# A sparse linear layer on one core: a new opening with six weight pieces, bf16 transposes and in-place pruning

## The chip, the core and the metric

The kernel runs on one core of one Trainium2 chip. The metric is device time in microseconds (us), the median over runs. Engines: TensorE (PE in the profile; its weight loads are listed apart as PEld), VectorE (DVE), ScalarE (ACT), GpSimd (POOL) and SyncE (SP). SyncE and ScalarE also issue the kernel's transfers, each from a queue of its own, in order.

## The reference

```python
B, S, D = 16, 512, 1024
x: (B, S, D) bf16;  w: (D, D) bf16;  b: (D,) bf16

def reference(x, w, b):
    G = D // 4
    wg = w.reshape(G, 4, D)
    mag = jnp.abs(wg)
    order = jnp.argsort(mag, 1)
    thr = jnp.take_along_axis(mag, order[:, 2:3, :], 1)
    mask = (mag >= thr)
    wp = (wg * mask).reshape(D, D)
    return jnp.einsum("bsd,df->bsf", x, wp) + b
```

In every group of four neighbouring rows of w, in each column, the two entries of largest magnitude stay (all that equal the second largest stay too), the others become zero. Then x times the pruned w, plus b. There are 8192 tokens, that is 64 tiles of 128; each tile needs 8 blocks of 128 contraction rows against 1024 output columns, so 16 matmuls of 512 columns.

## The kernel before

**Two layouts.** The rows of w are packed: partition q of half g (g is 0 or 1) holds rows 4q to 4q+3 of that half, as four slices m. So the four entries of a group lie in one partition and VectorE can compare them. The first 7 tiles of tokens are multiplied against this packed pruned weight `wp` while it is being made; this is the *opening*. The pruned weight is also written to a scratch tensor in memory (`save`, L183) and read back in natural row order (`reload`, L186); the other 57 tiles are multiplied against that `wp_nat`, with x brought in by transposing transfers (`load_batch`, L237). That is the *natural part* (L334 and L369). Its first batch, 5 tiles, runs all first output halves (h = 0) and then all second halves (h = 1), so the reload of the second half is wanted only at the sixth group of 8 matmuls.

**The opening.** The weight is pruned in pieces, each a half g and a range of columns, `pieces` (L123): seven, of 128, 128, 256, 256, 256, 512 and 512 columns. A piece takes eight steps: `abs`, `hi` and `lo` (larger and smaller of two pairs), `t1` (smaller of the larger two), `t2` (larger of the smaller two), `thr` (larger of these, the second largest of the four), `mask` (magnitude >= thr), `mult` (weight times mask, written to `wp`). VectorE does them (`Piece.do`, L161); the `abs` of some pieces is ScalarE's (`abs_act`, L158).

For a tile t and half g, `transpose` (L192) turns x with TensorE into PSUM, as fp32 words that hold two bf16 each: two fp32 transposes per tile and half. `copy_xt` (L201) has ScalarE bring it to SBUF. `mm_piece` (L209) then multiplies tile t with piece i, four matmuls (m = 0 to 3) that add up in a PSUM buffer of 512 columns for each tile and output half. `psum_o` has six such buffers, one of them first used by the fillers; `psum_t` has two for the transposes. `stage` (L224) copies a finished first half to SBUF on ScalarE and so frees its buffer; `finish` (L229) adds the bias to both halves on VectorE and stores the tile.

**What sets the order.** `seq` chains the instructions of each engine in the order in which they are emitted. Three lists written by hand, `order` (L249), give that order for TensorE, VectorE and ScalarE: T2a is the transpose of tile 2, half a; C2a its copy; M2.3 tile 2 with piece 3; F2 two filler matmuls on zeros; S2 the staging of tile 2; W5 the save of piece 5 from ScalarE's queue. `run` (L306) merges the lists: a token is emitted once those that it needs have been. Before the lists stand six fillers of 512 columns and three of 128 (L316).

SyncE's queue issues, in order: all early loads (L105 to L120), four saves, the transposed x of batch 0, both reloads, then further batches.

**Names.** x with a range, as `x_4_0` in load_x(4, 6, 0), is the load of tiles 4 and 5, half a.

Of the kernel before, what the change touches and what calls it, by code (L numbers as in the profile page):

```python
# [10 lines left out]
def kernel(  # L11
# [7 lines left out]
    nc = tc.nc  # L19
    P = 128  # L20
    bf16 = mybir.dt.bfloat16
# [11 lines left out]
    FH = 512  # L33
# [13 lines left out]

    const = ctx.enter_context(tc.tile_pool(name="const", bufs=1))
    dram = ctx.enter_context(tc.tile_pool(name="dram", bufs=1, space=bass.MemoryType.DRAM))
    wtmp = ctx.enter_context(tc.tile_pool(name="wtmp", bufs=2))  # L50
    xtp = ctx.enter_context(tc.tile_pool(name="xtp", bufs=NPK))
    stg = ctx.enter_context(tc.tile_pool(name="stg", bufs=NPK))
    xtb = ctx.enter_context(tc.tile_pool(name="xtb", bufs=3))
# [13 lines left out]
    def pe(i):  # L67
        return seq("pe", i)

    def dve(i):  # L70
        return seq("dve", i)

    def act(i):
        return seq("act", i)
# [3 lines left out]

    zeros = const.tile([P, P], bf16)
    dve(nc.vector.memset(zeros[:], 0.0))  # L80
    spark = const.tile([P, 1], bf16)


    w_sb = const.tile([P, G, 4, Dout], bf16)
# [9 lines left out]
    def load_w(g, c0, c1, eng="sp"):  # L94
        issue(eng, w_sb[:, g, :, c0:c1], wv[:, g, :, c0:c1])

    def load_x(ta, tb, g, eng="sp"):
        xs = const.tile([P, tb - ta, HK], bf16, name=f"x_{ta}_{g}")
        issue(eng, xs[:], xv[:, ta:tb, g * HK:(g + 1) * HK])
        for t in range(ta, tb):  # L100
            x_sb[(t, g)] = xs[:, t - ta, :]


    act(nc.scalar.activation(spark[:], zeros[:, :1], Act.Abs))
    load_w(0, 0, CW)  # L105
    load_x(0, 1, 0)
    load_x(1, 2, 0)
    load_x(2, 4, 0)
    load_w(0, CW, FH)
    load_x(4, 6, 0)  # L110
    load_w(1, 0, CW)
    load_x(0, 2, 1)
    load_x(2, 4, 1)
    load_x(6, 7, 0)
    load_w(1, CW, FH)
    load_x(4, 6, 1)
    load_x(6, 7, 1)
    load_w(0, FH, Dout)
    load_w(1, FH, Dout)
    sp(nc.sync.dma_start(bias_sb[:], b.partition_broadcast(P)))  # L120


    pieces = [(0, 0, P), (0, P, CW), (0, CW, FH), (1, 0, CW), (1, CW, FH), (0, FH, Dout), (1, FH, Dout)]  # L123

    ident = const.tile([P, P], fp32)
    make_identity(nc, ident[:])
    warm_ps = psum_o.tile([P, FH], fp32, name="ps")

    def filler(n, rep=1):
        for _ in range(n):  # L130
            pe(nc.tensor.matmul(warm_ps[:, :rep * P], lhsT=zeros[:],  # L131
                                rhs=zeros[:, None, :].to_broadcast([P, rep, P]), start=True, stop=True))
# [6 lines left out]

    class Piece:  # L140


        def __init__(self, i):
            self.g, self.c0, self.c1 = pieces[i]
            n = self.n = self.c1 - self.c0
            self.w = w_sb[:, self.g, :, self.c0:self.c1]
            self.mag = wtmp.tile([P, 4, FH], bf16, name="mag", bufs=5)[:, :, :n]
            self.hi = wtmp.tile([P, 2, FH], bf16, name="hi")[:, :, :n]
            self.lo = wtmp.tile([P, 2, FH], bf16, name="lo")[:, :, :n]
            self.t1 = wtmp.tile([P, FH], bf16, name="t1")[:, :n]  # L150
            self.t2 = wtmp.tile([P, FH], bf16, name="t2")[:, :n]
            self.thr = wtmp.tile([P, FH], bf16, name="thr")[:, :n]
            self.mask = wtmp.tile([P, 4, FH], bf16, name="mask")[:, :, :n]

        def tt(self, out, a, b_, op):
            dve(nc.vector.tensor_tensor(out, a, b_, op=op))  # L156

        def abs_act(self):  # L158
            act(nc.scalar.activation(self.mag, self.w, Act.Abs))  # L159

        def do(self, *steps):  # L161
            magv = self.mag.rearrange("p (a j) f -> p a j f", j=2)
            for step in steps:
                if step == "abs":
                    dve(nc.vector.tensor_single_scalar(
                        self.mag.bitcast(u16), self.w.bitcast(u16), 0x7FFF, op=Alu.bitwise_and))
                elif step == "hi":
                    self.tt(self.hi, magv[:, :, 0, :], magv[:, :, 1, :], Alu.max)
                elif step == "lo":
                    self.tt(self.lo, magv[:, :, 0, :], magv[:, :, 1, :], Alu.min)  # L170
                elif step == "t1":
                    self.tt(self.t1, self.hi[:, 0, :], self.hi[:, 1, :], Alu.min)
                elif step == "t2":
                    self.tt(self.t2, self.lo[:, 0, :], self.lo[:, 1, :], Alu.max)
                elif step == "thr":
                    self.tt(self.thr, self.t1, self.t2, Alu.max)
                elif step == "mask":
                    self.tt(self.mask, self.mag,
                            self.thr[:, None, :].to_broadcast([P, 4, self.n]), Alu.is_ge)
                else:  # L180
                    self.tt(wp[:, self.g, :, self.c0:self.c1], self.w, self.mask, Alu.mult)

    def save(g, c0, c1, eng="sp"):  # L183
        issue(eng, scr_pk[:, g, :, c0:c1], wp[:, g, :, c0:c1])
# [7 lines left out]
    def transpose(t, g):  # L192


        xg = x_sb[(t, g)].bitcast(fp32).rearrange("p (q u) -> p u q", u=2)
        tp = psum_t.tile([P, 2, P], fp32, name="tp")
        for u in range(2):
            pe(nc.tensor.transpose(tp[:, u, :], xg[:, u, :], ident[:]))  # L198
        xpk[(t, g)] = tp

    def copy_xt(t, g):  # L201
        xt = xtp.tile([P, 2, P], fp32, name=f"xt{g}")
        act(nc.scalar.copy(xt[:], xpk[(t, g)][:]))  # L203
        v = xt[:].bitcast(bf16).rearrange("p u (t v) -> p u v t", v=2)
        xpk[(t, g)] = [v[:, m // 2, m % 2, :] for m in range(4)]

    ps_open = {}

    def mm_piece(t, i):  # L209
        g, c0, c1 = pieces[i]  # L210
        h = c0 // FH
        new = (t, h) not in ps_open
        if new:
            ps_open[(t, h)] = psum_o.tile([P, FH], fp32, name="ps")
        ps = ps_open[(t, h)]
        for m in range(4):
            pe(nc.tensor.matmul(ps[:, c0 - h * FH:c1 - h * FH], lhsT=xpk[(t, g)][m],  # L217
                                rhs=wp[:, g, m, c0:c1],
                                start=(new and m == 0), stop=(g == 1 and m == 3),
                                skip_group_check=True))  # L220

    staged = {}
# [14 lines left out]
    def load_batch(bi):  # L237
# [5 lines left out]
        for j in range(nb):  # L243
# [4 lines left out]

    order = {  # L249
        "pe": (  # L250
            "T0a T1a F2 T2a T3a F2 M0.0 M1.0 M2.0 M3.0 T4a T5a M0.1 M1.1 M2.1 M3.1 M4.0 M4.1 T0b "
            "T1b M5.0 M5.1 T2b T6a M0.2 T3b M1.2 M2.2 T4b M3.2 T5b T6b M4.2 M5.2 M0.3 M1.3 M2.3 "
            "M3.3 M4.3 M5.3 M0.4 M1.4 M2.4 M3.4 M4.4 M5.4 M6.0 M6.1 M6.2 M6.3 M6.4 M0.5 M1.5 M2.5 "
            "M3.5 M4.5 M5.5 M0.6 M1.6 M2.6 M3.6 M4.6 M5.6 M6.5 M6.6"
        ),
        "dve": (
            "abs0 hi0 lo0 t10 t20 hi1 thr0 lo1 mask0 t11 mult0 t21 thr1 mask1 mult1 abs2 hi2 lo2 "
            "t12 t22 thr2 mask2 mult2 hi3 lo3 t13 t23 thr3 mask3 mult3 hi4 lo4 t14 t24 thr4 mask4 "
            "mult4 hi5 lo5 t15 t25 thr5 mask5 mult5 hi6 lo6 t16 t26 thr6 mask6 mult6"
        ),  # L260
        "act": (
            "abs1 C0a C1a C2a C3a C4a C5a abs3 C0b C1b C2b C6a abs4 C3b C4b C5b C6b abs5 abs6 S0 S1 "
            "S2 S3 S4 S5 W5 S6 W6"
        ),
    }
    written = set()
    p = {}

    def needs(eng, tok):

        if tok[0] == "C":
            return ["T" + tok[1:]]
        if tok[0] in "TF":
            return []
        if tok[0] == "M":
            t, i = tok[1:].split(".")
            return [f"C{t}{'ab'[pieces[int(i)][0]]}", f"mult{i}"]
        if tok[0] == "S":
            return [f"M{tok[1:]}.{i}" for i in range(5)]
        if tok[0] == "W":  # L280
            return ["mult" + tok[1:]]
        return ["abs" + tok[-1]] if tok[:-1] in ("hi", "mask") else []

    def emit(eng, tok):
        if tok[0] == "T":
            transpose(int(tok[1]), "ab".index(tok[2]))
        elif tok[0] == "F":
            filler(int(tok[1:]))
        elif tok[0] == "C":
            copy_xt(int(tok[1]), "ab".index(tok[2]))  # L290
        elif tok[0] == "M":
            mm_piece(*map(int, tok[1:].split(".")))
        elif tok[0] == "S":
            stage(int(tok[1:]))
        elif tok[0] == "W":
            save(*pieces[int(tok[1:])], eng="act")
        else:
            i = int(tok[-1])
            if i not in p:
                p[i] = Piece(i)  # L300
            if eng == "act":
                p[i].abs_act()
            else:
                p[i].do(tok[:-1])

    def run(queues):  # L306
        while any(queues.values()):
# [6 lines left out]
            assert moved, queues  # L314

    filler(6, 4)  # L316
    filler(3)
    run({eng: order[eng].split() for eng in order})
    save(0, 0, CW)
    save(0, CW, FH)  # L320
    save(1, 0, CW)
    save(1, CW, FH)
    load_batch(0)
    reload(0)
    reload(1)
    load_batch(1)
    load_batch(2)
    for t in range(NPK):
        finish(t)


# [76 lines left out]
```

## Time and profile before

| what | value |
|---|---|
| median of 4 runs | 237.25 us (236.18 to 238.4) |
| profiled execution | 236.18 us, span 234.4 us |
| TensorE busy | 228.0 us, 97% of the span |
| VectorE busy | 104.7 us, 45% |
| ScalarE busy | 15.8 us, 7% |
| granted TensorE clock | 1.000 |
| first pruning step, first opening matmul | 3.92 us, 7.03 us |
| first matmul of the natural part | 34.70 us |
| last product of the pruning ready | 26.96 us |
| second reload issued | 32.16 us |

Times inside the run count from the start of the span. A matmul's listed duration reaches from its issue to its modelled end, so neighbours overlap: a 512-wide one is listed with 379 ns while they start 216 ns apart. What TensorE can do is therefore read from the distance of starts, and the share of busy time says only that it hardly waits. A row such as `L198 PE MATMUL tp<-ident,x 128*128 128x128 f32 x28` names line, engine, operation, the tile written and the tiles read, and how many there are.

### The profile page before, as it was taken

How to read it: one execution, taken by the hardware profiler on the slowest of the kernel's cores; microseconds unless marked ns; L12 is line 12 of the kernel's file. 1: busy time of each engine (PE TensorE's matmuls, PEld its weight loads, DVE VectorE, ACT ScalarE, POOL GpSimd, SP SyncE). 2: the span in 40 equal slices, each digit the busy share in tenths (PEclk: the TensorE clock that was granted, in tenths of full speed). 3: DMA queues.
4: the chain of work that ended last, by engine and by line, in shares of the span. 5: the costliest groups of instructions: out<-in, count | busy, mean ns of one | idle time of the engine just before them, and what ended most of it. 6: DMA issues, size and time to landing. Idle time of an engine off the chain costs nothing.

```text
span 234.4 us, 2830 instructions
## 1 busy us (share of the span) xinstructions
PE 228.0 (97%) x1145; PEld 112.2 (48%) x1165; DVE 104.7 (45%) x182; ACT 15.8 (7%) x28; POOL 0.7 (0%) x6
## 2 busy tenths in 40 slices
PE   6899999999999999999999999999999999999995
PEld 3898444444444444444444444444444444444443
DVE  3989697342442442343343244234334324424424
ACT  4588000000000000000000000000000000000000
POOL 1000000000000000000000000000000000000000
PEclk9999999999999999999999999999999999999999
DMA  5999969999999712892219912595221221222122
GB/s 157 316 348 249 339 195 329 313 297 249 262 277 221 241 72 89 206 286 92 89 60 215 301 65 78 117 277 187 92 91 45 89 91 50 86 89 88 49 90 90
DMA packets 79500, 40.29 MB, mean 172 GB/s; under 512 B 60416, under 2 KB 71936, under 8 KB 79488
## 3 DMA queue, kind: packets, MB, share of 16 engines
q1 hardware_dynamic: 68352, 22.45, 43.7%
q10 hardware_dynamic: 11136, 17.67, 21.1%
q8 instruction: 9, 0.15, 0.3%
q14 instruction: 3, 0.02, 0.0%
HBM read 6.29 MB, written 18.87 MB: 107 GB/s over the span
## 4 chain that ended last, share of the span: by engine, by line
PE 95%; DMA 2%; SPq 1%; issue 1%; DVE 0%
PE ps L369 75%; PE ps L217 10%; PE ps L334 9%; DMA x<-in_x_dram 2%; PE tp L198 1%; SPq L92 1%; DVE o L338 0%
## 5 line engine op out<-in xcount | busy, mean ns | idle before, releaser
L369 PE MATMUL ps<-wp_nat,xb 128*128 128x512 bf16 x800 | 175.4, 379 | 0.8
L338 DVE TENSOR_TENSOR o<-ps,bias_sb 128x512 bf16<-128x512 f32 (+1 forms) x116 | 74.3, 678 | 120.5 <-PE ps L369 103.9
L369 PEld LDWEIGHTS <-xb 128*128 128x128 bf16 x816 | 79.9, 98 | 96.3
L217 PE MATMUL ps<-wp,xt 128*128 128x256 bf16 (+2 forms) x194 | 25.4, 287 | 0.1
L334 PE MATMUL ps<-wp_nat,xb 128*128 128x512 bf16 (+2 forms) x110 | 21.0, 348 | 0.1
L217 PEld LDWEIGHTS <-xt 128*128 128x128 bf16 x196 | 17.1, 98 | 7.3
L334 PEld LDWEIGHTS <-xb 128*128 128x128 bf16 x112 | 10.4, 98 | 10.7
L198 PE MATMUL tp<-ident,x 128*128 128x128 f32 x28 | 5.4, 302 | 1.7 <-DMA x<-in_x_dram 1.7
L159 ACT ACTIVATE mag<-w_sb 128x1024 bf16<-128x1024 bf16 (+2 forms) x5 | 6.5, 1317 | 1.7 <-DMA w_sb<-in_w_dram 1.7
L231 DVE TENSOR_TENSOR o<-ps,bias_sb 128x512 bf16<-128x512 f32 x7 | 4.8, 685 | 1.9 <-PE ps L217 1.9
L156 DVE TENSOR_TENSOR mask<-mag,thr 128x1024 bf16<-128x1024 bf16 (+2 forms) x7 | 5.4, 768 | 0.2
L156 DVE TENSOR_TENSOR wp<-w_sb,mask 128x1024 bf16<-128x1024 bf16 (+2 forms) x7 | 5.4, 767 | 0.2
L198 PEld LDWEIGHTS tp<-ident,x 128*128 128x128 f32 x28 | 4.1, 206 | 2.4 <-issue 1.5
L203 ACT COPY xt<-tp 128x256 f32<-128x256 f32 x14 | 4.7, 375 | 4.2 <-PE tp L198 4.2
L232 DVE TENSOR_TENSOR o<-st,bias_sb 128x512 bf16<-128x512 f32 x7 | 4.8, 682 | 0.0
L131 PE MATMUL ps<-zeros 128*128 128x128 bf16 (+1 forms) x13 | 3.6, 430 | 1.0 <-DVE zeros L80 1.0
L226 ACT COPY st<-ps 128x512 f32<-128x512 f32 x7 | 3.6, 608 | 0.9 <-PE ps L217 0.9
L156 DVE TENSOR_TENSOR hi<-mag 128x512 bf16<-128x512 bf16 (+2 forms) x7 | 3.2, 459 | 0.5 <-ACT mag L159 0.5
L156 DVE TENSOR_TENSOR lo<-mag 128x512 bf16<-128x512 bf16 (+2 forms) x7 | 3.2, 457 | 0.0
L131 PEld LDWEIGHTS <-zeros 128*128 128x128 bf16 x13 | 1.6, 130 | 2.7 <-issue 1.7
L156 DVE TENSOR_TENSOR thr<-t,t 128x256 bf16<-128x256 bf16 (+2 forms) x7 | 2.2, 310 | 0.2
L156 DVE TENSOR_TENSOR t<-hi 128x256 bf16<-128x256 bf16 (+2 forms) x7 | 2.1, 304 | 0.0
(11 smaller groups left out, 5.3 us busy)
## 6 DMA issues: line engine op xcount, KB each, us to landing
out_dram<-o ACTq DMA_DIRECT2D x58, 256.0 KB, 3.0
wp_nat<-wp_scratch SPq DMA_DIRECT2D x2, 1024.0 KB, 7.3
x<-in_x_dram SPq DMA_DIRECT2D x5, 256.0 KB, 5.1
out_dram<-o ACTq DMA_DIRECT2D x10, 128.0 KB, 1.7
w_sb<-in_w_dram SPq DMA_DIRECT2D x4, 256.0 KB, 4.4
w_sb<-in_w_dram SPq DMA_DIRECT2D x2, 512.0 KB, 6.6
wp_scratch<-wp SPq DMA_DIRECT2D x4, 256.0 KB, 6.7
wp_scratch<-wp ACTq DMA_DIRECT2D x2, 512.0 KB, 4.9
```

The lines of the kernel that those rows point to most:

```text
L131: pe(nc.tensor.matmul(warm_ps[:, :rep * P], lhsT=zeros[:], rhs=zeros[:, None, :].to_broadcast([P, rep, P]), start=True, stop=True))
L156: dve(nc.vector.tensor_tensor(out, a, b_, op=op))
L159: act(nc.scalar.activation(self.mag, self.w, Act.Abs))
L198: pe(nc.tensor.transpose(tp[:, u, :], xg[:, u, :], ident[:]))
L203: act(nc.scalar.copy(xt[:], xpk[(t, g)][:]))
L217: pe(nc.tensor.matmul(ps[:, c0 - h * FH:c1 - h * FH], lhsT=xpk[(t, g)][m], rhs=wp[:, g, m, c0:c1], start=(new and m == 0), stop=(g == 1 an ...
L226: act(nc.scalar.copy(st[:], ps_open.pop((t, 0))[:]))
L231: dve(nc.vector.tensor_tensor(o[:, FH:], ps_open.pop((t, 1))[:], bias_sb[:, FH:], op=Alu.add))
L232: dve(nc.vector.tensor_tensor(o[:, :FH], staged.pop(t)[:], bias_sb[:, :FH], op=Alu.add))
L334: pe(nc.tensor.matmul(ps, lhsT=xt[:, kt, :], rhs=wp_nat[:, kt, c0:c1], start=(kt == 0), stop=(kt == KT - 1)))
L338: dve(nc.vector.tensor_tensor(o[:, c0:c1], ps, bias_sb[:, c0:c1], op=Alu.add))
L369: pe(nc.tensor.matmul(pss[h][:], lhsT=xt[:, kt, :], rhs=wp_nat[:, kt, h * FH:(h + 1) * FH], start=(kt == 0), stop=(kt == KT - 1)))
```

## The change

Only the opening is changed; the natural part's code is the same.

- **Pieces.** Six: (0, 0-256), (0, 256-512), (1, 0-256), (1, 256-512), (0, 512-1024), (1, 512-1024), as half and columns. The first one's `mask`, `mult` and matmuls are split into x (slices m = 0, 1) and y (m = 2, 3).
- **Transposes.** Four bf16 transposes of 128 columns for each tile and half (x read with a step of four elements) in place of two fp32 ones; the identity is bf16; ScalarE copies the same bytes, and the matmuls read contiguous weights in place of a step of two.
- **In-place pruning.** `t1`, `t2`, `thr` overwrite `hi` and `lo`, and `mask` overwrites the magnitudes. Each piece has its own buffers.
- **Orders.** New lists for the three engines, in other tile order (6, 5, 4, 3, 2, 1, 0), with more fillers (8 in place of 3 ahead of the lists, then 5, 6 and 7); `abs` of pieces 0 and 1 on VectorE, of the others on ScalarE, piece 3 pruned ahead of piece 2; the saves of the two large pieces both last on ScalarE's queue. `run` also respects the buffers that a token needs.
- **Loads.** All on the SP queue as before, in a new order and with x in other groups.
- **Finishing.** The tiles are finished in the order 2, 0, 3, 1, 6, 5, 4.

```diff
-    act(nc.scalar.activation(spark[:], zeros[:, :1], Act.Abs))
-    load_w(0, 0, CW)
+    load_w(0, 0, 256)
+    for _ in range(1):
+        act(nc.scalar.activation(spark[:], zeros[:], Act.Abs))
+    load_x(6, 7, 0)
+    load_x(4, 6, 0)
+    load_x(2, 4, 0)
+    load_w(0, 256, 512)
+    load_x(6, 7, 1)
+    load_x(1, 2, 0)
+    load_w(1, 256, 512)
+    load_x(2, 4, 1)
+    load_w(1, 0, 256)
+    load_x(4, 6, 1)
+    load_w(0, 512, 1024)
+    load_x(0, 2, 1)
     load_x(0, 1, 0)
-    load_x(1, 2, 0)
-    load_x(2, 4, 0)
-    load_w(0, CW, FH)
-    load_x(4, 6, 0)
-    load_w(1, 0, CW)
-    load_x(0, 2, 1)
-    load_x(2, 4, 1)
-    load_x(6, 7, 0)
-    load_w(1, CW, FH)
-    load_x(4, 6, 1)
-    load_x(6, 7, 1)
-    load_w(0, FH, Dout)
-    load_w(1, FH, Dout)
+    load_w(1, 512, 1024)
...
-    pieces = [(0, 0, P), (0, P, CW), (0, CW, FH), (1, 0, CW), (1, CW, FH), (0, FH, Dout), (1, FH, Dout)]
+    pieces = [(0, 0, 256), (0, 256, 512), (1, 0, 256), (1, 256, 512), (0, 512, 1024), (1, 512, 1024)]
 
-    ident = const.tile([P, P], fp32)
+    ident = const.tile([P, P], bf16)
...
+            elif step == "t1":
+                self.tt(hi[:, 0, :], hi[:, 0, :], hi[:, 1, :], Alu.min)
+            elif step == "t2":
+                self.tt(lo[:, 0, :], lo[:, 0, :], lo[:, 1, :], Alu.max)
+            elif step == "thr":
+                self.tt(thr, hi[:, 0, :], lo[:, 0, :], Alu.max)
+            elif step == "mask":
+                self.tt(self.mag[:, ms, :], self.mag[:, ms, :],
+                        thr[:, None, :].to_broadcast([P, n, self.n]), Alu.is_ge)
+            else:
+                self.tt(wp[:, self.g, ms, self.c0:self.c1], self.w[:, ms, :], self.mag[:, ms, :], Alu.mult)
...
-        xg = x_sb[(t, g)].bitcast(fp32).rearrange("p (q u) -> p u q", u=2)
-        tp = psum_t.tile([P, 2, P], fp32, name="tp")
-        for u in range(2):
-            pe(nc.tensor.transpose(tp[:, u, :], xg[:, u, :], ident[:]))
+        xg = x_sb[(t, g)].rearrange("p (q m) -> p m q", m=4)
+        tp = psum_t.tile([P, 4, P], bf16, name="tp")
+        for m in range(4):
+            pe(nc.tensor.transpose(tp[:, m, :], xg[:, m, :], ident[:]))
         xpk[(t, g)] = tp
 
     def copy_xt(t, g):
-        xt = xtp.tile([P, 2, P], fp32, name=f"xt{g}")
-        act(nc.scalar.copy(xt[:], xpk[(t, g)][:]))
-        v = xt[:].bitcast(bf16).rearrange("p u (t v) -> p u v t", v=2)
-        xpk[(t, g)] = [v[:, m // 2, m % 2, :] for m in range(4)]
+        xt = xtp.tile([P, 4, P], bf16, name=f"xt{g}")
+        act(nc.scalar.copy(xt[:].bitcast(fp32), xpk[(t, g)][:].bitcast(fp32)))
+        xpk[(t, g)] = [xt[:, m, :] for m in range(4)]
...
         "pe": (
-            "T0a T1a F2 T2a T3a F2 M0.0 M1.0 M2.0 M3.0 T4a T5a M0.1 M1.1 M2.1 M3.1 M4.0 M4.1 T0b "
-            "T1b M5.0 M5.1 T2b T6a M0.2 T3b M1.2 M2.2 T4b M3.2 T5b T6b M4.2 M5.2 M0.3 M1.3 M2.3 "
-            "M3.3 M4.3 M5.3 M0.4 M1.4 M2.4 M3.4 M4.4 M5.4 M6.0 M6.1 M6.2 M6.3 M6.4 M0.5 M1.5 M2.5 "
-            "M3.5 M4.5 M5.5 M0.6 M1.6 M2.6 M3.6 M4.6 M5.6 M6.5 M6.6"
+            "T6a F5 T5a T4a F6 T3a T2a F7 M5.0y M4.0y M6.0y M2.0y M5.0x M3.0x T6b T1a M6.0x M3.0y "
+            "M4.0x M2.0x M1.0y M1.0x T3b T2b M6.1 M4.1 M3.1 T4b M1.1 M5.1 T5b M2.1 M6.3 M3.3 M4.3 "
+            "T1b T0b M5.3 M2.3 M1.3 M3.2 M6.2 M5.2 T0a M4.2 M2.2 M1.2 M0.0y M0.1 M0.2 M0.3 M0.0x "
+            "M2.4 M3.4 M1.4 M0.4 M5.4 M4.4 M5.5 M2.5 M1.5 M4.5 M6.4 M0.5 M6.5 M3.5"
         ),
         "dve": (
-            "abs0 hi0 lo0 t10 t20 hi1 thr0 lo1 mask0 t11 mult0 t21 thr1 mask1 mult1 abs2 hi2 lo2 "
-            "t12 t22 thr2 mask2 mult2 hi3 lo3 t13 t23 thr3 mask3 mult3 hi4 lo4 t14 t24 thr4 mask4 "
-            "mult4 hi5 lo5 t15 t25 thr5 mask5 mult5 hi6 lo6 t16 t26 thr6 mask6 mult6"
+            "abs0 hi0 lo0 t10 t20 thr0 mask0y mask0x mult0y abs1 mult0x hi1 lo1 t11 t21 thr1 mask1 "
+            "mult1 lo3 hi3 t23 t13 thr3 mask3 mult3 lo2 hi2 t22 t12 thr2 mask2 mult2 lo4 hi4 t24 "
+            "t14 thr4 mask4 mult4 hi5 lo5 t25 t15 thr5 mask5 mult5"
         ),
         "act": (
-            "abs1 C0a C1a C2a C3a C4a C5a abs3 C0b C1b C2b C6a abs4 C3b C4b C5b C6b abs5 abs6 S0 S1 "
-            "S2 S3 S4 S5 W5 S6 W6"
+            "C6a C5a C4a C2a C3a C6b C1a abs3 C3b abs2 C2b C4b C5b abs4 C1b abs5 C0a S5 C0b S1 S4 "
+            "S6 S2 S0 S3 W5 W4"
         ),
...
     filler(6, 4)
-    filler(3)
+    filler(8)
...
-    for t in range(NPK):
+    for t in (2, 0, 3, 1, 6, 5, 4):
         finish(t)
```

## The prediction, made before the changed kernel ran

> **What bounds the kernel now.** I read the page's first part, then the chain that ended last in order of time, then the timeline of the first 35 us and the queue's issues with their times to landing. The first part says which engine counts:
>
> ```profile
> PE 228.0 (97%) x1145; PEld 112.2 (48%) x1165; DVE 104.7 (45%) x182; ACT 15.8 (7%) x28; POOL 0.7 (0%) x6
> ```
>
> The chain (start us, length us, what) says where TensorE joins the chain and what runs in the opening:
>
> ```profile
> 3.69 4.71 DMA x<-in_x_dram
> 8.40 0.14 issue
> 8.53 0.72 PE tp L198 x4
> 9.25 1.34 PE ps L217 x24
> 10.59 0.53 PE tp L198 x4
> ...
> 12.83 0.87 PE ps L217 x8
> ...
> 33.84 1.03 PE ps L217 x4
> 34.86 9.71 PE ps L334 x45
> ```
>
> After 8.5 us nothing but TensorE is on it. The last opening matmul hands over to the natural-order part (L334) with its first matmul at 34.70 in the timeline, and from there to the end 57 tiles run back to back, at 0.2158 us a 512-wide matmul (10.74 + 0.05 us for 50). The diff leaves that part alone, so **the change is worth what it does to the 34.70**, provided that nothing later comes to wait.
>
> From these rows come the paces, start to start: 0.056 us for a 128-wide bf16 matmul (1.34/24), 0.108 for a 256-wide one (0.87/8), 0.137 for an fp32 transpose (two a tile half; 0.53 to 0.56 for four). Of what TensorE does from 8.53 to 34.70: 40 matmuls of 128 columns (2.24), 84 of 256 (9.07), 56 of 512 (12.08), 20 transposes (2.74): 26.13 of 26.17 us. It is dense.
>
> Who feeds it:
>
> ```profile
> 7.59 0.42 DVE L165 TENSOR_SCALAR mag<-w_sb 128x1024 uint16<-128x1024 uint16 x1
> 10.29 0.69 DVE L156 TENSOR_TENSOR wp<-w_sb,mask 128x1024 bf16<-128x1024 bf16 x1
> 10.90 0.42 DVE L156 TENSOR_TENSOR hi<-mag 128x512 bf16<-128x512 bf16 x1
> 17.16 0.69 DVE L156 TENSOR_TENSOR hi<-mag 128x1024 bf16<-128x1024 bf16 x1 [0.46 <-ACT mag L159]
> 22.02 0.68 DVE L156 TENSOR_TENSOR hi<-mag 128x1024 bf16<-128x1024 bf16 x1
> 25.73 1.23 DVE L156 TENSOR_TENSOR wp<-w_sb,mask 128x2048 bf16<-128x2048 bf16 x1
> 26.98 0.52 ACTq L92 DMA_DIRECT2D wp_scratch<-wp  x1
> ```
>
> Two lines of one kind give the cost of a piece on VectorE. A 256-column piece: 0.45 us for the abs and 2.86 from its first max to the next piece's first (10.90 to 13.76 for the one after), its product ready 2.95 after the first. A 512-column piece: 4.86 (17.16 to 22.02), ready after 4.95. The last product is done at 26.96. Eight 512-wide groups follow it (8 x 0.863 = 6.9), so VectorE could have allowed a hand-over at 33.9: before, TensorE binds by 0.8 us.
>
> **The change, part by part.** I follow the new chain from the first load; times are those of the profiled run.
>
> *Loads.* From issue and time to landing, the landings before are, by KB issued up to then: 256 at 3.9 us, 384 at 4.2, 512 at 5.4, 768 at 6.2, 1024 at 7.0, 1280 at 8.4, 1536 at 9.25, 1792 at 10.05, 2432 at 12.0, 2688 at 12.8, 3328 at 14.7, 3840 at 16.2. The same bytes go out in another order, so I read the new landings off this curve: first weights 3.9, x6 4.2, x4-5 5.8, x2-3 6.6, the second weight block (1152 KB) 7.7, x6's other half 8.4, x1 8.8, third weights 9.65, fourth 11.1, large weights 13.55 and 16.2, tiles 0 and 1 14.3 to 14.7. The one that matters is 7.7. It is bounded by 7.3 and 8.1, half a step of the curve each way.
>
> *First piece on VectorE.* 256 columns at once rather than 128 plus 128: abs at 3.92, first max 4.37, six steps later the first half-product is written 6.56 to 6.98. (Splitting mask and product in two costs nothing: independent 512-element steps follow each other at 0.33 to 0.34, and four make 1.33, as long as the undivided pair.) In-place operands keep the same chain of waits; they are free because VectorE runs in order anyway, and if each did cost 0.05 us, five a piece would delay products by 0.25 a piece. In the queue behind it stands abs1, ahead of the second half-product: it waits for the load at 7.7, and that product is ready at 8.57 instead of about 7.3.
>
> *Before the first matmul.* The transposes of tiles 3 and 2 wait for 6.6 and for ScalarE's copies (0.33 apart), then 7 fillers of 0.056; the first matmul starts near 7.65 (before: 7.03). The y halves (8 x 0.108) end at 8.5, the x halves at 8.62 find their product. With 16 transposes among them the 24 matmuls of piece 0 would end near 11.3. Piece 1: abs1 7.7, first max 8.49, ready 11.44. So **TensorE takes up piece 1 at about 11.48, held by the load at 7.7 through VectorE**; the later first matmul and the fillers are hidden by this wait, and would cost 0.4 if it were gone.
>
> *From there on.* Left are 88 matmuls of 256 columns (7 tiles x 16 less 24; 9.50), 56 of 512 (12.08), and 20 bf16 transposes. These are the only new operation. By the nearest row, 128-wide bf16 matmuls with their weight loads, one takes 0.056 to 0.059 (24 loads in 1.45 us):
>
> ```profile
> 8.97 1.45 PEld L217 LDWEIGHTS <-xt 128*128 128x128 bf16 x24
> 11.41 0.72 PE L198 MATMUL tp<-ident,x 128*128 128x128 f32 x4
> ```
>
> [...] What the row doesn't cover is the step: the transpose loads x with a column step of 4 bf16 (8 bytes), while the weights of L217 have a step of 2. [...] Upper end: the fp32 row, 0.137 each, 2.74. Lower end: a quarter of the 512-wide pace, 0.054.
>
> Sum: 11.48 + 9.50 + 12.08 + 1.15 = **34.2, against 34.70: 0.5 us sooner**. Is anything later? Piece starts on VectorE are 11.35, 14.21, 17.07, 21.93; products at 14.3, 17.2, 22.0, 26.9 are wanted at 14.5, 17.6, 22.1, 27.3: all covered, by 0.1 to 0.4. ScalarE's abs of pieces 3 and 2 (1.07) and 4 and 5 (1.91) end 11.2, 12.7, 16.5, 18.8, before VectorE asks. Its staging copies (0.6 each) come 0.2 ahead of their slots. VectorE's floor, 26.9 + 6.9 = 33.8, is 0.4 below.
>
> *Behind the opening.* The sync queue's third save now waits for the later of the two pieces (17.2 instead of 13.9) and holds the fourth, the first transposed x load and both reloads behind it: these start 0.9 later (18.3 and 24.3), the first reload lands near 31.5, wanted at 34.2. On ScalarE's queue the two large saves now both follow the last product (26.95, 27.5); one used to leave at 22.13. 512 KB more at about 330 GB/s is 1.6 us: saves landed near 33.6 (before 32.06), second reload (7.7) 41.3, wanted by the sixth group at 34.2 + 8.63 = 42.8. The new order of the output adds frees a buffer for the first natural group after tile 0's add, whose matmuls end 1.7 us before the hand-over: no wait.
>
> **Rivals.** [...] *Late loads.* abs1 blocks VectorE, and every us that the second weight block lands after 7.7 goes to the hand-over: from 8.2 on the gain is gone; 9.0 gives 238.0. For it: between 1024 and 1280 KB the curve stood for 1.4 us. *The second reload* (the one on the other side): should the two late saves land one after the other, each 5.1 as the last did, they end at 37.7, the reload lands at 45.5 and TensorE stands 2.7 us in front of the sixth group: 239.4. It decides from a landing of both saves after 35.1. Against it: the engines were only 63% busy from 30 to 32 us. *It doesn't do what it says*: the weights land early, fillers and order don't matter, and the hand-over is within 0.2 of before: 237.2. *More gain*: with the block at 7.0, and products ahead, TensorE is bound by its first matmul: 33.8; with x landing sooner too, 33: 235.5.
>
> **The numbers.** Median 237.25 less 0.5 gives **236.7**; the profiled execution, 236.18 with 1.8 us around its span, would become 235.7. Forecast 235.9 to 237.1: 0.53. More gain 0.13, strided 0.12, late loads 0.10, second reload 0.12. 1% (2.4 us) is about what a measurement of this kernel can tell from no change; past it lie 0.06 of the gains and 0.08 of the losses (mostly the reload). The range, 235.2 to 238.5, leaves out the far ends of these.
>
> **What would show it.** The changed profile should have: bf16 transposes at about 0.23 us for four; VectorE idle 0.7 to 0.8 in front of the second abs, put down to the weight load; the first L334-like matmul at 34.2; no idle time of TensorE at the sixth natural group. The prediction is wrong if the hand-over is after 34.9 or TensorE stands anywhere after it.

## The result: half a microsecond, as forecast, with landings that the forecast had not read

The changed kernel takes 236.38 us (median of 36 runs, 235.71 to 240.75), the kernel before 236.94 (57 runs, 236.18 to 238.56). The ratio is 0.9984 with a 95% interval of 0.9972 to 0.9996, so the change gains 0.1 to 0.7 us. That is less than the 1% (2.4 us) that the prediction took as what a measurement can tell; still, a ratio of 1 lies outside the interval. The ratio (0.4 us) weighs all the fast runs, some of them well above the median in the changed kernel, so it is less than the 0.56 us between the medians. The forecast was 236.7.

| | before | after |
|---|---|---|
| median | 236.94 us | 236.38 us |
| lowest run | 236.18 us | 235.71 us |
| profiled execution, span | 236.18 us, 234.4 us | 236.16 us, 234.4 us |
| first opening matmul | 7.03 us | 8.35 us |
| last product ready | 26.96 us | 27.34 us |
| hand-over to the natural part | 34.70 us | 34.67 us |

The two profiled executions hardly differ, although the medians do: the profile of before is its lowest run, the one of after lies near its median. Lowest to lowest is 0.47 us, median to median 0.56. So the profile of after is read for where its time is, and not subtracted from the other one.

The page's first part and two of its groups, after (line, engine, operation, tiles, count, then busy time, mean ns of one, idle time before it and what ended that):

```profile
PE 228.3 (97%) x1164; PEld 112.8 (48%) x1184; DVE 104.4 (45%) x177; ACT 15.3 (7%) x27; POOL 0.7 (0%) x6
...
L195 PE MATMUL tp<-ident,x 128*128 128x128 bf16 x56 | 4.8, 224 | 1.4 <-DMA x<-in_x_dram 1.4
...
L195 PEld LDWEIGHTS <-x 128*128 128x128 bf16 x56 | 4.2, 117 | 1.6 <-DMA x<-in_x_dram 1.5
```

TensorE fills the span as before. The 56 new transposes are there, with one stop of 1.4 us, for x, in front of the second group of them.

The chain that ended last, after (start us, length us, what):

```profile
2.14 4.40 DMA x<-in_x_dram
...
6.58 0.64 PE tp L195 x8
7.22 0.34 PE ps L132 x6
7.56 0.56 PE tp L195 x8
8.12 0.39 PE ps L132 x7
8.51 1.31 PE ps L220 x12
9.82 0.45 PE tp L195 x8
...
34.84 9.71 PE ps L360 x45
```

The chain leaves the loads at 6.54, when x of tiles 4 and 5 lands (before: at 8.40, for another x), and is TensorE alone from there, the fillers (L132) included. Eight bf16 transposes between matmuls take 0.45 us, 0.056 each.

The timeline of after (start us, duration us, engine, line, what; in brackets the idle time before and what ended it):

```profile
8.16 0.43 DVE L162 TENSOR_SCALAR mag<-w_sb 128x1024 uint16<-128x1024 uint16 x1 [1.27 <-DMA w_sb<-in_w_dram]
...
8.35 1.47 PE L220 MATMUL ps<-wp,xt 128*128 128x256 bf16 x12
...
11.86 1.47 PE L220 MATMUL ps<-wp,xt 128*128 128x256 bf16 x12
...
33.40 0.38 SPq L185 DMA_DIRECT2D wp_nat<-wp_scratch  x1
33.82 11.30 SPq L245 DMA_TRANSPOSE xb<-in_x_dram  x1
34.67 1.67 PE L360 MATMUL ps<-wp_nat,xb 128*128 128x512 bf16 x7
```

VectorE stood 1.27 us for the second weight block; piece 1's product was ready at 11.77 and TensorE, still busy, took it up at 11.86. So in this run TensorE was not held there as the prediction had it, though it missed that by only 0.09 us. The last product is done at 27.34, and both large saves leave right then. The second reload is issued at 33.40 (before 32.16), behind it in the same queue the x of the second batch (33.82; before 32.59).

One rule reads most of the profiles below: hand-over plus 199.7 us is the span (34.67 + 199.7 = 234.4; before 34.70 + 199.7 = 234.4), to 0.1 us in nearly all, unless TensorE stands later on (*hand-over* is the first matmul of the natural part).

### The profile page after: what moved, and what is told of

The parts are those of the page before. It is cut to its first block, busy times and chain, and to the rows that moved or that the text cites. A ratio compares the mean times of both kernels' runs of the same rounds, so it can differ in the third digit from the quotient of the medians.

```text
span 234.4 us, 2851 instructions
## 1 busy us (share of the span) xinstructions
PE 228.3 (97%) x1164; PEld 112.8 (48%) x1184; DVE 104.4 (45%) x177; ACT 15.3 (7%) x27; POOL 0.7 (0%) x6
## 4 chain that ended last, share of the span: by engine, by line
PE 96%; DMA 2%; issue 1%; SPq 1%; DVE 0%
PE ps L395 75%; PE ps L220 10%; PE ps L360 9%; DMA x<-in_x_dram 2%; PE tp L195 1%; SPq L92 1%; PE ps L132 0%; DVE o L364 0%
## 5 line engine op out<-in xcount | busy, mean ns | idle before, releaser
L220 PE MATMUL ps<-wp,xt 128*128 128x256 bf16 (+1 forms) x166 | 25.4, 307 | 0.1
L360 PEld LDWEIGHTS <-xb 128*128 128x128 bf16 x112 | 10.4, 98 | 10.7
L195 PE MATMUL tp<-ident,x 128*128 128x128 bf16 x56 | 4.8, 224 | 1.4 <-DMA x<-in_x_dram 1.4
L132 PE MATMUL ps<-zeros 128*128 128x128 bf16 (+1 forms) x32 | 5.1, 320 | 1.0 <-DVE zeros L80 1.0
L155 ACT ACTIVATE mag<-w_sb 128x1024 bf16<-128x1024 bf16 (+1 forms) x4 | 6.0, 1492 | 0.0
L152 DVE TENSOR_TENSOR wp<-w_sb,mag 128x1024 bf16<-128x1024 bf16 (+2 forms) x7 | 5.4, 766 | 0.2
L152 DVE TENSOR_TENSOR mag<-mag,hi 128x1024 bf16<-128x1024 bf16 (+2 forms) x7 | 5.3, 767 | 0.2
L195 PEld LDWEIGHTS <-x 128*128 128x128 bf16 x56 | 4.2, 117 | 1.6 <-DMA x<-in_x_dram 1.5
L132 PEld LDWEIGHTS <-zeros 128*128 128x128 bf16 x32 | 2.8, 120 | 2.6 <-issue 1.6
L152 DVE TENSOR_TENSOR hi<-mag 128x512 bf16<-128x512 bf16 (+1 forms) x6 | 3.0, 508 | 0.0
L152 DVE TENSOR_TENSOR lo<-mag 128x512 bf16<-128x512 bf16 (+1 forms) x6 | 3.1, 509 | 0.0
L152 DVE TENSOR_TENSOR hi<-hi,lo 128x256 bf16<-128x256 bf16 (+1 forms) x6 | 2.0, 337 | 0.2
```

The lines of the kernel that those rows point to most:

```text
L132: pe(nc.tensor.matmul(warm_ps[:, :rep * P], lhsT=zeros[:], rhs=zeros[:, None, :].to_broadcast([P, rep, P]), start=True, stop=True))
L155: act(nc.scalar.activation(self.mag[:], self.w, Act.Abs))
L195: pe(nc.tensor.transpose(tp[:, m, :], xg[:, m, :], ident[:]))
L360: pe(nc.tensor.matmul(ps, lhsT=xt[:, kt, :], rhs=wp_nat[:, kt, c0:c1], start=(kt == 0), stop=(kt == KT - 1)))
```

## The experiments

The first six ask what sets the hand-over. **Theory 1** is a TensorE bound by its first matmul, so by x and the fillers; **Theory 2**, the prediction's, is a TensorE held at piece 1 by the second weight block through VectorE, with the fillers hidden by that wait. The later ones ask where the runs above 237.4 us come from (the *upper runs*: 10 of the changed kernel's 36, 9 of 57 before), with **Theory A** for the late saves, and which version is best. Ratios are to the kernel before, timed on the same chip; the changed kernel's is 0.9984 (0.9972 to 0.9996).

### The transposes undone, and the transposes alone

```diff
-    ident = const.tile([P, P], bf16)
+    ident = const.tile([P, P], fp32)
...
-        xg = x_sb[(t, g)].rearrange("p (q m) -> p m q", m=4)
-        tp = psum_t.tile([P, 4, P], bf16, name="tp")
-        for m in range(4):
-            pe(nc.tensor.transpose(tp[:, m, :], xg[:, m, :], ident[:]))
+        xg = x_sb[(t, g)].bitcast(fp32).rearrange("p (q u) -> p u q", u=2)
+        tp = psum_t.tile([P, 2, P], fp32, name="tp")
+        for u in range(2):
+            pe(nc.tensor.transpose(tp[:, u, :], xg[:, u, :], ident[:]))
```

ScalarE's copy and the step of the matmuls' weights go back with it.

> The changed kernel with the fp32 transposes of before (two a tile half, same copies). Theory 1, TensorE's own work from its first opening matmul sets the hand-over: the nine tile halves transposed after it cost 0.275 us each again in place of 0.226, 0.44 us in all, hand-over 35.1 to 35.2, ratio to before about 1.000 to 1.001 (the change itself 0.9984). Theory 2, VectorE and the weight loads set it: TensorE has slack, hand-over stays at 34.7, ratio 0.998.

Measured: 237.97 us, ratio 1.0013 (0.9984 to 1.0041); profiled 238.06 us, span 236.3. The hand-over is at 35.00, 0.33 later: 0.20 of it is the first matmul (8.55), behind slower transposes. It lies between the two theories' (35.1 to 35.2 and 34.7), and the ratio is not told from the changed kernel's. But hand-over plus 199.7 is 234.7, not 236.3. The waits of TensorE from 30 to 80 us (us in total, times, longest) say where the rest is:

```profile
PE ps L396 <- DMA xb<-in_x_dram: 1.4, 1, 1.4
```

and the chain that ended last of the same kernel how it comes about:

```profile
28.21 6.07 DMA wp_scratch<-wp
...
34.34 0.38 SPq L185
...
34.77 19.01 DMA xb<-in_x_dram
...
53.83 3.41 PE ps L396 x15
```

The last save's landing releases the second reload (L185), and behind the reload in SP's queue the second batch's x, which took 19.01 us to land and came 1.4 us late. The reload itself was in time. The same transfer and its first use, in the kernel before and in the changed kernel:

```profile
32.59 9.72 SPq L242 DMA_TRANSPOSE xb<-in_x_dram  x1
51.97 2.32 PE L369 MATMUL ps<-wp_nat,xb 128*128 128x512 bf16 x10
```

```profile
33.82 11.30 SPq L245 DMA_TRANSPOSE xb<-in_x_dram  x1
51.94 2.32 PE L395 MATMUL ps<-wp_nat,xb 128*128 128x512 bf16 x10
```

In the changed kernel's profile that x took 16.2 us to land, at 50.0, so it had 1.9 us of slack; in the kernel before it took 13.7, landed at 46.3, and had 5.7.

The other way round, the kernel before with nothing but the bf16 transposes (the diff above backwards, in the kernel before):

> The kernel before with nothing changed but the transposes: four bf16 ones a tile half in place of two fp32, contiguous copies. Ten halves are transposed after TensorE becomes dense: at 0.056 us a transpose they take 2.26 in place of 2.74, hand-over 34.2 in place of 34.70, ratio 0.998; VectorE has 0.8 us of slack there and follows. [...] If first matmul and loads alone decide: 34.7, 1.000.

Measured: 236.44 us, ratio 0.9971 (0.9956 to 0.9986), so 0.3 to 1.0 us faster, with no run above 237.21 in 22. Its profiled run had TensorE at half pace until 9.7 us, so its hand-over (35.19) is not compared; from the same 24 matmuls on it is. The chain, transposes alone:

```profile
10.07 1.34 PE ps L216 x24
11.41 0.45 PE tp L198 x8
...
12.30 0.45 PE tp L198 x8
...
13.19 0.22 PE tp L198 x4
...
14.29 0.22 PE tp L198 x4
...
14.95 0.45 PE tp L198 x8
```

The transposes add up to 1.79 us; in the chain of before the same ones are 0.53, 0.56, 0.27, 0.23 and 0.53, together 2.12. The 0.33 less is all of the difference from there to the hand-over (35.19 - 10.07 = 25.12; before 34.70 - 9.25 = 25.45). So the transposes alone carry a gain as large as the whole change's. The traced 0.33 is about half of the 0.7 us of the ratio; what the rest is was not traced. What the new pieces, orders, loads and fillers add is not told from nothing: with bf16 transposes the ratios are 0.9971 without them and 0.9984 with them, and with fp32 transposes 1 and 1.0013, intervals overlapping both times. In this profile the second batch's x took 17.1 us as well (33.22 to 50.35), so a long landing there does not need the new orders.

### Fewer and more fillers

```diff
-            "T6a F5 T5a T4a F6 T3a T2a F7 M5.0y ...
+            "T6a F5 T5a T4a F2 T3a T2a M5.0y ...
```

> The changed kernel without the seven fillers ahead of the first opening matmul and with two in place of six before them. Theory 2, VectorE behind the second weight load sets the hand-over, as predicted: nothing gained, hand-over within 0.1 of the changed kernel's, TensorE stands idle in front of the second half-product or of piece 1 instead. Theory 1, the first matmul sets it: it starts 0.39 us sooner and the hand-over with it, 34.3, ratio to before 0.9968.

Measured: 237.1 us, ratio 0.9983 (0.9962 to 1.0003). The first matmul comes 0.33 earlier, at 8.02, the hand-over only 0.09, at 34.58. The chain with fewer fillers:

```profile
3.10 4.98 DMA w_sb<-in_w_dram
...
8.11 0.43 DVE mag L162
...
11.77 1.47 PE ps L220 x12
```

It now runs from the second weight load (landed 8.08) through VectorE's piece 1 to the matmuls at 11.77: what the prediction named as the wait that hides the fillers.

```diff
-            "T6a F5 T5a T4a F6 T3a T2a F7 M5.0y ...
+            "T6a F5 T5a T4a F6 T3a T2a F14 M5.0y ...
```

> The changed kernel with fourteen fillers in place of seven ahead of the first matmul, 0.39 us more. Theory 1: hand-over 0.39 later, 35.06, ratio to before 1.000. Theory 2: hidden by the wait for piece 1, hand-over 34.7, ratio 0.998.

Measured: 236.88 us, ratio 0.9986 (0.9958 to 1.0014). In its profile (237.04 us) x landed 0.5 later too, the first matmul started at 9.21 and the hand-over is 35.53. That is the first matmul plus 26.32, and in the changed kernel it is 34.67 - 8.35 = 26.32 as well. With fewer fillers it is 34.58 - 8.02 = 26.56: 0.24 of waiting. So in these profiles both theories hold within 0.1 us of each other: the first matmul binds by that much, and the weight block is next. Neither timed ratio is told from the changed kernel's; the theories are told apart by the profiles alone.

### The second weights ahead of x

```diff
-    load_x(2, 4, 0)
     load_w(0, 256, 512)
+    load_x(2, 4, 0)
```

> The changed kernel with the second weight block loaded ahead of tiles 2 and 3. The weights land near 7.5 us in place of 8.1, the x near 8.1 in place of 7.5. Theory 1, the first matmul (behind this x) sets the hand-over: 0.6 later, 35.3, ratio 1.001. Theory 2, VectorE sets it: up to 0.6 sooner, 34.1 to 34.3, ratio 0.996 to 0.997.

Measured: 238.36 us, ratio 1.0038 (1.0018 to 1.0058): 0.4 to 1.4 us slower, more than either theory has. In its profile the second weights land at 7.97 in place of 8.13, so they gain 0.16, while x of tiles 2 and 3 lands at 8.69 in place of 7.30, and TensorE stands for it. The stop, and the window behind it (granted clock third from the end, DMA share and GB/s behind it):

```profile
8.74 1.04 PE L195 MATMUL tp<-ident,x 128*128 128x128 bf16 x8 [0.59 <-DMA x<-in_x_dram]
9.00:10.00 1.00, 1.00 (x12) 1.00 (x10) 0.97 (x5) 0.18 (x1) 0.00 (x0) 0.50 1.07 325
```

The trace records the clock at 0.50 from 8.73 to 12.15 us, 3.41 us, which alone makes a mean clock of 0.993 over the run (0.991 is listed, with a short stretch at the very end). The first matmul (10.32) is late for both reasons. Every timed run lists its mean clock: 11 of these 22 have 0.991 to 0.993 and a median of 238.77 us, the other 11 have 0.999 or 1.000 and 237.57. So moving the weights forward costs more than it gives, in part through x and in part through the clock, which falls in more of the runs (8 of 59 in the kernel before, timed beside it, and 4 of the changed kernel's 37).

### The first x loads on ScalarE's queue

```diff
+    load_x(6, 7, 0, "act")
+    load_x(4, 6, 0, "act")
+    load_x(2, 4, 0, "act")
     for _ in range(1):
         act(nc.scalar.activation(spark[:], zeros[:], Act.Abs))
-    load_x(6, 7, 0)
-    load_x(4, 6, 0)
-    load_x(2, 4, 0)
```

> The changed kernel with the first three x loads issued from ScalarE's queue beside the first weights. If the low rate between 3.5 and 5 us (98 to 168 GB/s) comes from waiting for issue or from one queue's order, x lands 0.5 to 1 us sooner, the second weights too, and the hand-over is 33.7 to 34.3, ratio 0.994 to 0.997. If it comes from the transfers themselves, the first weights land up to 0.5 later, the others as now: hand-over 34.6 to 35.1, ratio 0.998 to 1.000.

Measured: 235.79 us, ratio 0.9945 (0.9924 to 0.9966), 10 runs, none above 236.32; profiled 235.82, hand-over 34.34. The windows of half a microsecond show that the loads are better off (busy time and count of each engine, granted clock, DMA share, GB/s last); the changed kernel, then this one:

```profile
3.50:4.00 0.50, 0.50 (x6) 0.48 (x5) 0.20 (x1) 0.00 (x0) 0.00 (x0) 1.00 0.70 111
4.00:4.50 0.50, 0.50 (x8) 0.50 (x6) 0.47 (x2) 0.00 (x0) 0.00 (x0) 1.00 1.24 98
```

```profile
3.50:4.00 0.50, 0.50 (x6) 0.48 (x5) 0.00 (x0) 0.33 (x2) 0.00 (x0) 1.00 0.82 248
4.00:4.50 0.50, 0.50 (x12) 0.50 (x10) 0.00 (x0) 0.00 (x0) 0.00 (x0) 1.00 0.75 236
```

Behind the first weights, on one queue, the rate in the changed kernel's profile falls to 111 and 98 GB/s for a microsecond; in this one, on two queues, it does not fall below 236 from 3.0 to 6.5 us. In return the first weights land 1.1 us later (4.84), and in the timeline TensorE's first opening matmul (8.00) waits 0.16 us for their product instead. The loads were also issued sooner, x at 0.74 to 1.65 us in place of 1.48 to 2.60 and the second weights at 1.49 in place of 3.11, so the issue time saved and the order on two queues are not told apart. The ratio lies 0.4% below the changed kernel's, some 0.9 us; 0.33 of it is the earlier hand-over. The upper runs are missing, which may be the rest.

### One large save earlier

```diff
-            "S6 S2 S0 S3 W5 W4"
+            "S6 S2 W4 S0 S3 W5"
```

> The changed kernel with the save of piece 4 four steps earlier on ScalarE's queue, behind the fourth staging copy (about 23 us in place of 27.9); only one large save still follows the last product, as before. Theory A, the two late saves push back the second reload and with it the transposed x of the second batch, which then comes late in some runs: the second reload is issued near 32.3 in place of 33.4, that x lands 1 to 3 us sooner, no run is held at the second batch, the runs above 237.4 go, and the median falls by 0.2 to 0.5, ratio to before 0.995 to 0.997. Theory B, those runs come from load landings in the opening: nothing changes, ratio 0.998, the same upper runs.

Measured: 236.31 us, ratio 0.9983 (0.9962 to 1.0005). The save left at 22.15 instead of 27.4, and yet the second batch's x was issued at 33.65 (33.82 in the changed kernel) and took 16.2 us again. 3 of 14 runs still lie above 237.4. What the second reload waits for is the last save, and that one did not come sooner (landed at 33.16; 33.33 in the changed kernel); the other one beside it cost nothing that can be seen. So the x did not come sooner, as Theory A needed, and this run leaves that theory open. The profile (235.86 us, hand-over 34.37) shows something else: with the same load order x of tiles 4 and 5 was there at 5.77, the second weights at 7.58, and the first matmul at 7.54.

### Combinations on two queues

With the x loads, the early save and the fewer fillers of above in one kernel:

> The kernel with three x loads on ScalarE's queue, the early save, no fillers ahead of the first matmul and two in place of six before. The first product (7.95) held its first matmul, so fillers gain nothing; with the save early nothing comes late: hand-over 34.2 to 34.4, ratio 0.993 to 0.995.

Measured: 235.69 us, ratio 0.9949 (0.9930 to 0.9969), hand-over 34.22. The same, but with the three x loads emitted behind ScalarE's first activation, so that they are issued beside its table load, from 0.97 us:

> As the one before, but the three x loads are issued from ScalarE behind its table load, so from about 2.3 us. The first weights land near 3.8 again in place of 4.9, x near 6.5 to 7, the second weights sooner than 7. If the first matmul sets the hand-over it starts near 7.3 and the hand-over is 33.5 to 33.9, ratio 0.990 to 0.993; if the loads only change places it is 34.3 and 0.994.

Measured: 236.35 us, ratio 0.9978 (0.9954 to 1.0003), hand-over 34.54, 6 of 18 runs above 237.4: a miss, since neither branch had the hand-over above 34.3. The first weights come sooner (4.2), x of tiles 2 and 3 only at 7.7. Five of the six upper runs list a mean clock of 0.992 or 0.993; none of the 10 runs of the two-queue kernel above does. The two intervals overlap, so it is likely but not shown that x has to be the first thing on the second queue.

### The second batch's x ahead of the second reload

```diff
     reload(0)
-    reload(1)
     load_batch(1)
+    reload(1)
```

> The changed kernel with the transposed x of the second batch issued ahead of the second reload in place of behind it. Theory A, runs above 237.4 are held at the second batch because its x lands late behind the second reload: that x now lands near 40 in place of 50, no run is held there, the upper runs go; the reload is issued near 35 and lands 42 to 43.5, just at its use (43.3), so up to 0.5 us may be lost at the sixth group in its place; ratio to before 0.996 to 0.999. Theory B, the upper runs have nothing to do with the second batch: as many of them stay.

Measured: 245.57 us, ratio 1.0357 (1.0320 to 1.0394): a clear miss. The waits of TensorE from 30 to 80 us:

```profile
PE ps L360 <- DMA wp_nat<-wp_scratch: 8.0, 1, 8.0
```

The second reload was issued at 43.11, nearly 10 us later than in the changed kernel (33.40), since it waits for the saves. These were issued from ScalarE's queue at 27.4 and 28.0, as always, but now behind the second batch's transposing transfer (issued at 25.34, landed at 42.45), and landed about 15 us later instead of 5. A transposing transfer in flight is not always enough for that: in the kernel before, a save of the same size issued at 22.13, beside batch 0's (17.29 to 27.07), took 4.7 us. Of the 10.4 us by which the profiled run is longer than the changed kernel's, 8.0 are the stop; behind it the clock is lower for a while, 0.50 from 45.8 to 56.05 us in the trace, of which TensorE worked 4.6 us at half pace and so lost about 2.3. Giving the second batch its slack this way takes it from the reload, and more; of Theories A and B this run tells nothing.

### The order of finishing

```diff
-    for t in (2, 0, 3, 1, 6, 5, 4):
+    for t in (5, 2, 1, 4, 0, 6, 3):
```

> The changed kernel with the opening's tiles finished in the order in which their matmuls end (5, 2, 1, 4, 0, 6, 3) in place of 2, 0, 3, 1, 6, 5, 4. The output stores leave from 29.5 us on in place of 31, the last near 36.5 in place of 41, so fewer of them lie beside the second reload and the second batch's x. Theory A1, these stores delay that x: it takes 14 us to land in place of 16.2, the upper runs become fewer than 1 in 7, ratio 0.996 to 0.998. Theory A2, the later issue alone (33.8 in place of 32.6) does it: no change, ratio 0.998, upper runs as before.

Measured: 236.19 us, ratio 0.9966 (0.9951 to 0.9982), which is not told from the changed kernel. The second batch's x took 14.7 us (35.48 to 50.13), as Theory A1 has it, and with the later hand-over had over 3 us of slack; whether that makes the upper runs fewer (1 of 10) was not told. The profiled run was its slowest, 237.55 us, and shows one kind of upper run. Its chain:

```profile
6.54 1.04 PE tp L195 x8
7.58 0.64 PE ps L132 x6
8.22 0.85 PE tp L195 x8
9.08 0.75 PE ps L132 x7
```

x landed at 6.54 as in the changed kernel's profile, but TensorE needs 1.04, 0.64, 0.85 and 0.75 us for what took it 0.64, 0.34, 0.56 and 0.39: half pace until 9.8 us. The same matmuls start 107 ns apart there in the trace and 56 behind it. The first matmul is 1.3 late (9.62), the hand-over 1.4 (36.07), and the time 1.4 (237.55 against 236.16). Nothing stands later. The view lists the granted clock as 1.00 in those rows, but only because the trace holds no clock record there: its first one begins at 9.86 us, at full clock, where the pace changes. In the profile with the second weights first, 107 ns is the pace at a recorded 0.50. So, by its pace, TensorE was at half clock until then. Every profile begins so: the first 512-column fillers start 427 ns apart, against 216 later. The change comes between about 4 and 7 us in twelve of the fourteen profiles, and at 9.7 and 9.9 us in the one with the transposes alone and this one. So the moment varies by almost 6 us over these profiles; what sets it was not shown.

With this order on top of the two-queue kernel:

> The kernel with three x loads on ScalarE's queue, the early save and few fillers, and the tiles finished in the order in which they are done. If the stores beside the second batch's x cost anything in typical runs, ratio below that kernel's 0.9949, near 0.993 to 0.994; if they cost nothing there, 0.995, hand-over again 34.2 to 34.4.

Measured: 235.74 us, ratio 0.9941 (0.9920 to 0.9961); not told from the two other kernels with x first on ScalarE's queue. The hand-over of its profile (236.32 us) is 34.82, later than forecast, because the first weights landed at 5.33 (4.72 in the kernel without this order). The second batch's x took 12.9 us in place of 17.3, which bought no time that can be told. Of the 26 runs of these three none lies above 236.66.

## Why the prediction was right

**What it had right.** The sum was 0.5 us of the time before; 0.56 is between the medians, 0.4 by the ratio. The term that paid for it was the transposes, 0.275 to 0.23 us a tile half: measured 0.225, and alone worth 0.3 to 1.0 us. The sum's 1.15 us for the last 20 of them was the author's estimate, 0.0575 each, since the profile of before has no bf16 transpose; in the changed kernel's chain those 20 take 0.22, 0.22, 0.45 and 0.22 us, together 1.11, so 0.056 each, weight load included, and the column step of 8 bytes lost nothing of the row's 0.056 to 0.059. The weight loads do last a little longer, 113 against 98 ns (117 in the group's mean, which takes in the first four at half pace, 152 each), and hide. VectorE's rows carried over: pieces of 2.89 and 4.86 us (2.86 and 4.86 forecast), so the in-place operands cost nothing. No TensorE stop at the sixth natural group, and the second reload landed at 40.2, with 3 us to spare. The hand-over of 34.67 is below the 34.9 that the prediction named as the sign of being wrong.

**Right in part: the wait at piece 1.** The prediction had TensorE held there by the second weight block, with the fillers hidden. In the changed kernel's profile TensorE was bound by its first matmul, by 0.09 us; with the fillers taken away the hold appears, and 0.09 is gained of the 0.33 by which the first matmul moved. So most of the fillers' time was hidden, and the two paths were almost even.

**What was mis-sized: the landings of the early loads.** Read off the curve of before they were 5.8, 6.6 and 7.7 for x of tiles 4-5, of 2-3, and the second weights; the profile of after has 6.5, 7.3 and 8.1, the last just outside the 7.3 to 8.1 that was given as its bound. VectorE's wait for it was 1.27 us and not 0.7 to 0.8, the first matmul 8.35 and not 7.65, piece 1 taken up at 11.86 and not 11.48, hand-over 34.67 and not 34.2. Had this run stood for all, the gain would have been nil, as the late-loads rival said for a landing from 8.2 on. It does not stand for all: with an unchanged load order the second weights came at 7.6 in one profile and at 8.0 to 8.5 in six, x of tiles 4-5 at 5.7 in two and at 6.5 to 7.0 in five. The step's fault was to take one run's curve for a value with half a step of error, when it is a spread of a microsecond; and the profile from which 0.5 was subtracted was itself the fastest of 57. The two errors, each of about the size of the whole gain, stood against each other. That the median came out where the sum had it is so far luck; the transposes' term is not, since it was measured alone.

**The rivals.** Slower strided transposes, to which the prediction gave 0.12, are excluded by the pace of 0.056 us each. "More gain" needed the second weights at 7.0, and no profile with the changed kernel's load order has them before 7.55. The second reload did not come late, but the rival was near: the next transfer in the same queue, the second batch's x, had 3.8 us less slack in this profile than in that of before, and in one profiled kernel TensorE stood 1.4 us for it. The prediction had not followed that transfer.

**What stays open.** The upper runs have at least three causes that the record shows: half clock into the opening's matmuls, and the second batch's x, at 1.4 us each in a profile; and a clock that falls back for a while. The runs' mean clocks tell of the last. Four of the changed kernel's 10 upper runs list 0.992 or 0.993 (237.83 to 240.75 us), and every other of its runs 0.999 or 1.000. A stretch of 3.41 us at half clock, as traced with the second weights first, makes a mean of 0.993 and costs up to 1.7 us (an estimate: half of it). How the other six divide was not measured, nor why the clock falls. The 26 runs with x first on ScalarE's queue list none below 0.999. TensorE's pauses ahead of the first matmul do not sort the kernels by it: the longest is 1.37 us in the changed kernel's profile and 0.56 to 0.98 in those three, but 0.97 in the one with x behind the table load, where 5 of 18 runs fell.

## What to carry to other kernels

When an opening is dense on its engine, look for a cheaper form of what is on the chain; here the change of the transposes alone gave no less than the whole rewritten opening, as far as the intervals tell. Follow every transfer that stands behind a moved one in its queue to its own consumer, not only the first one. Take landing times from several runs: one trace gave them to about a microsecond, twice the gain in question. And list the mean clock of every run before explaining a spread: here it sorts out four of ten upper runs at once.

## What the runs showed of the hardware that was not expected

- On one queue, in the changed kernel's profile, x behind the first weights came at 98 to 168 GB/s from 3.5 to 5.0 us (90 to 125 from 3.5 to 4.5 in the kernel before); with x first on a second queue the rate was 236 to 282 in one profile and 252 to 284 in another, but 153 and 222 from 3.5 to 4.5 in the third, with the same loads in the same order.
- With the second batch's transposing transfer (17 us to its landing) issued 2 us ahead of them from another queue, two plain saves lasted 14.4 and 15.1 us instead of about 5. Batch 0's did not do that to the save beside it in the kernel before (4.7 us).
- TensorE begins every profile at the pace of half clock (427 ns for a 512-column matmul against 216 later, 107 for one of 128 against 56) and changes to the full pace at about 4 to 7 us, in two of fourteen at 9.7 and 9.9. The view prints 1.00 where the trace has no clock record.
- With the second weights first, the clock fell back to 0.50 for 3.41 us (8.73 to 12.15) with no pause of TensorE longer than 1.65 us before it.
